# A two-branch mixer on one core: where V rows land, how the attention output comes back, who begins the first loads, and fused feature maps

## The chip, the cores and the metric

The kernel runs on one core of one Trainium2 chip. The metric is the device time of one execution in microseconds. A core has five instruction streams that run side by side and meet through semaphores: TensorE (PE, matmuls into PSUM), VectorE (DVE), ScalarE (ACT), GpSimd (POOL) and SyncE (SP), which in this kernel issues the DMAs.

## The reference

Two branches read the same input `x` of 2048 tokens by 512 channels, and a gate per token mixes them. Everything is bfloat16 at the borders.

```python
g = sigmoid((x * gate_w).sum(-1, keepdims=True))
a = A(x)          # 32 heads of 16, four segments of 512 tokens
b = B(x)          # a long convolution per channel
return g * a + (1 - g) * b

# A, for segment s of 4:  phi(t) = where(t > 0, t + 1, exp(t))
p     = softmax(q_s k_s^T * scale + causal_mask)
a_mem = (phi(q_s) @ M) / (phi(q_s) @ z + 1e-6)
o_s   = sigmoid(beta) * a_mem + (1 - sigmoid(beta)) * (p @ v_s)
M, z  = M + phi(k_s)^T v_s,  z + phi(k_s).sum()
# then all segments' o @ wo

# B:  K[d, l] = Re sum_n C[d,n] * exp(dt*A[d,n]*l) * dt*B[d,n]
y = irfft(rfft(x, 2L) * rfft(K, 2L))[:L] + x * Dskip
```

## The kernel before

The kernel is built by a planner in Python. Functions such as `project`, `group`, `ophase`, `oproj`, `tables` and `tail` hand operations to a class `Sched`, each with an engine, a modelled cost, the tiles that it reads and writes and a priority key. `Sched.schedule` then builds one fixed order for each engine: it takes, among the operations that could start now, the one with the lowest key. Keys come from the constants `KEYS` and, for single stages by name, from `ORDER`. Some PSUM evacuations may go to ScalarE or VectorE (`evac`, lines 264 to 273), and `PEN` is added to the key for VectorE; `MODEK` is added for a change of TensorE's tile shape. `VPK` is the packet count that the planner charges for a V transfer. `Sched.emit` writes the streams out, with a wait wherever one engine needs another's result. So a change of a constant can move any operation of the program.

Buffers are pools at fixed SBUF addresses with a phase number. Pools of different phases may overlap; a pool can be used once every overlapping pool of an earlier phase has given back all of its tiles.

The work, in its order:

- **Loads and prologue.** All DMAs are issued by SP, one after the other: the parameters of branch B, `x` of segment 0, then `wq`, `wk`, `wv`. TensorE transposes parameters and `x`; `ssm_prep` and `ssm_powers` build powers of exp(dt*A) on VectorE and ScalarE.
- **Attention, four segments of four head groups.** `project` makes q and k, `key_tokens` and `seg_state` the state M (with the feature map of k as two terms, min(exp, 1) and max(k, 0), that are both multiplied with v), `group` the masked softmax, `ophase` the normalised result, with the memory term from segment 1 on. For the last segment (`LATEO = 12`) the two terms of phi(q) are added inside `ophase` (line 1181). `oproj(s)` multiplies by `wo`, scales by the gate (lines 269 and 270), and writes four row blocks of 128 tokens to a DRAM scratch `scr_abuf`. Two buffers `ag` hold the rows on their way.
- **Tables of branch B.** `table_f` and `tables` (VectorE, lines 1250 to 1255) build the kernel K in the tiles `F` and `G` with a scratch `t2`; each chunk goes through a DRAM scratch `scr_K`.
- **Convolution.** `x_level1` does the first level of a transform of `x` and stores it in a DRAM scratch `scr_Z`; `tail` loads it as four tiles `Zx`. For each of 16 frequency groups t, `tail` loads constants `c_D` (tile `Dst`, five buffers), transforms K (matmuls from line 1333), transforms x (line 1344), multiplies on VectorE (lines 1351 to 1358), transforms back into a tile `V` (line 1366) and sends V by a DMA from SBUF to SBUF into eight partitions of the large tile `V2`. These are the "K steps".
- **Final stage.** For each of 16 output column blocks, six matmuls give the last level plus the skip term, and VectorE adds the gated attention tile `aj` (line 1395, `SCALAR_TENSOR_TENSOR`). `aj` is read back from `scr_abuf` in four loads of 512 KB. Five output writes follow.

The V transfer and the read-back, before:

```python
S.dma(lambda t=t: sbp(V2, t, 16, 8, [[1024, 16], [1, 1024]]), ...)      # partitions t, t+16, ..., t+112
S.dma(lambda aj=aj: ap(aj, n=2048),
      lambda gq=gq: bass.AP(abuf, gq * 2048, [[8192, 128], [1, 2048]]), ...)
```

Of the kernel before, what the change touches and what calls it, by code (L numbers as in the profile page):

```python
# [8 lines left out]
BF16 = mybir.dt.bfloat16  # L9
# [8 lines left out]
VPK = 1400  # L18
LATEM, LATEO = 24, 12
MODEK = 3.2  # L20
PEN = 8.8
SHOW = 0
KEYS = (11.73, 0.11, 49.7, 49.9, 6.68, 12.43, 50.14, 14.66, 16.9, 95.49, 11.41, 2.82)
NDST, NV = 5, 5
ORDER = {'grp0.3.1': 5.2, 'oph3.2': -34.8, 'ktok1.1': 7.8, 'grp0.0.0': 12.9, 'K1': 4.1, 'ktok2.0': -13.6, 'K8': -1.8, 'oph2.0': 21.1, 'grp0.0.1': 7.6, 'ktok2.1': -2.1, 'grp3.0.1': 8.5, 'grp3.3.1': -2.0, 'tabF': 3.5, 'tab3': 13.2, 'oph2.1': -3.4, 'oproj2': 9.3, 'oph3.3': -2.3, 'grp0.1.1': 0.3, 'tok3': -4.8, 'proj3.2': 0.5, 'proj2.2': -2.6, 'oph1.1': -20.1, 'grp3.1.0': 17.6, 'proj0.1': -9.4, 'state2': 38.3, 'ktok1.3': -3.1, 'state1': -12.4, 'oph1.0': 5.3, 'grp2.0.1': 0.6, 'oproj1': -9.3, 'proj1.1': -4.6, 'grp0.2.1': -1.7, 'K15': -3.7, 'ktok0.1': 1.3, 'proj1.3': -1.4, 'grp1.2.1': -8.6, 'grp3.0.0': 3.2, 'grp2.2.0': 3.1, 'proj3.0': -24.4}
# [109 lines left out]
class Op:  # L135
    __slots__ = ("eng", "cost", "fn", "deps", "key", "tiles", "wt", "nd", "succ", "start", "fin", "idx", "inc",
                 "val", "sem", "know", "waits", "seq", "lat", "alld", "tag", "alts", "pew", "mode", "base")


class Sched:  # L140
# [59 lines left out]
    def op(self, eng, cost, fn, r=(), w=(), pw=(), key=None, lat=None, acq=(), alts=None, pew=(), mode=None):  # L200
        o = Op()
        o.pew = pew
# [56 lines left out]
    def dma(self, out, in_, nbytes, r=(), w=(), pw=(), key=None, slow=False, packets=0):  # L259
        kw = {"allow_slow_non_contiguous": True} if slow else {}  # L260
        lat = max(nbytes / 290e3, packets * 0.0015)
        return self.op("SP", 0.4, lambda e: e.dma_start(out(), in_(), **kw), r=r, w=w, pw=pw, key=key, lat=lat)  # L262
# [178 lines left out]
    def emit(self):  # L441
# [49 lines left out]
        def make(e):  # L491
            def run(eng):
                for o in self.prog[e]:
# [8 lines left out]
                    if e == "SP":  # L502
                        ins.then_inc(dsem[o.sem[1]], 16)
                    elif o.inc:
                        ins.then_inc(sems[e], 1)
# [38 lines left out]
def fft_consts():  # L544
# [31 lines left out]
    for tp in range(32):  # L576
        for i in range(4):
            r = 16 * (4 * (tp % 2) + i) + tp // 2
# [31 lines left out]
def build_kernel(nc, A_x, A_wq, A_wk, A_wv, A_wo, A_beta, B_A_re, B_A_im, B_B_re, B_B_im,  # L610
                 B_C_re, B_C_im, B_log_dt, B_Dskip, gate_w, out):
    with contextlib.ExitStack() as es:
# [119 lines left out]
        DP = mkpool("Dst", 4096, NDST, 2)  # L732
        K3P = mkpool("K3", 2048, 3, 2)
        XsP = mkpool("Xs", 2048, 3, 2)
        YP = mkpool("Y", 2048, 3, 2)
        V2P = mkpool("V2", 32768, 1, 2)
        ZxP = [mkpool("Zx0", 8192, 1, 2)]
        VP = mkpool("V", 2048, NV, 2)
        assert a <= 207 * 1024, a
        a = A0  # L740
        ZxP += [mkpool("Zx1", 8192, 3, 2)] * 3
        TtP = mkpool("Tt", 2048, 2, 2)
        assert a <= E1, (a, E1)
        a = Q0
        ajP = mkpool("aj", 4096, 4, 2)
# [28 lines left out]
        for T, wsrc, ky in ((wqT, A_wq, 0.3), (wkT, A_wk, 0.4), (wvT, A_wv, 0.5), (woT, A_wo, 9.0)):  # L774
            S.dma(lambda T=T: ap(T, dims=[[512, 4], [1, 512]]), lambda wsrc=wsrc: wsrc.rearrange("(k p) n -> p k n", p=128),
                  524288, w=[T], key=ky)
# [10 lines left out]
        def do_xT(s):  # L787
# [4 lines left out]
                  524288, w=[xks], key=(-0.95 if s == 0 else S.key - 8))  # L792
# [102 lines left out]
        dA = [DT() for _ in range(16)]  # L895
# [85 lines left out]
        def key_tokens(s, hg):  # L981
# [10 lines left out]
            op("ACT", c_act(512), lambda e: e.activation(ap(ek, n=512), ap(P, n=512), ACT.Exp), r=[P], w=[ek])  # L992
            op("ANY", 0.0, None, r=[P], w=[rk], alts={
# [5 lines left out]
        def seg_state(s, hp):  # L999
# [3 lines left out]
            for _ in range(1):  # L1003
                P = S.ps()
                for h2 in range(2):
                    hg = 2 * hp + h2

                    def f(e, P=P, hg=hg, h2=h2):
                        for tb in range(4):
                            for wi in range(2):  # L1010
                                i = mm(e, ap(P, h2 * 136, n=136), ap(ekr[(s, hg)][wi], tb * 128, n=128),
                                       ap(vpad[s], tb * 544 + hg * 136, n=136), tb == 0 and wi == 0, tb == 3 and wi == 1)
                        return i
                    op("PE", c_mm(136, 8), f, r=[vpad[s]] + list(ekr[(s, hg)]), pw=[P], acq=[Mx[s + 1]])
# [10 lines left out]
        def project(s, hg):  # L1025
# [27 lines left out]
            if s > 0:  # L1053
                eq, rq = Tile(eqP, BF16), Tile(rqP, BF16)
                op("ACT", c_act(512), lambda e: e.activation(ap(eq, n=512), ap(qT, n=512), ACT.Exp), r=[qT], w=[eq])  # L1055
                op("DVE", c_ts4(512), lambda e: e.tensor_scalar_min(ap(eq, n=512), ap(eq, n=512), 1.0), w=[eq])
                op("DVE", c_ts4(512), lambda e: e.tensor_scalar_max(ap(rq, n=512), ap(qT, n=512), 0.0), r=[qT], w=[rq])
# [99 lines left out]
        def ophase(s, hg):  # L1157
# [18 lines left out]
            if s > 0:  # L1176
# [3 lines left out]
                if late:  # L1180
                    op("DVE", c_tt(512), lambda e: e.tensor_tensor(ap(eq, n=512), ap(eq, n=512), ap(rq, n=512), ALU.add), r=[rq], w=[eq])
# [30 lines left out]

        def oproj(s):
            S.tag = "oproj%d" % s
            ot = [oTs[(s, hg)] for hg in range(4)]
            for tb in range(4):
# [10 lines left out]
                S.dma(lambda tbg=tbg: abuf[128 * tbg:128 * tbg + 128, :], lambda ag=ag: ap(ag, n=512), 131072, r=[ag], w=[dA[tbg]])  # L1227
# [78 lines left out]
        def tail(k0):  # L1306
# [16 lines left out]
            for t in range(16):  # L1323
                S.key = k0 + 4 + KEYS[4] * t
                S.tag = "K%d" % t
                Dt = Tile(DP, BF16)
# [34 lines left out]
                V = Tile(VP, BF16)  # L1361
# [8 lines left out]
                S.dma(lambda t=t: sbp(V2, t, 16, 8, [[1024, 16], [1, 1024]]), lambda V=V: ap(V, n=1024), 262144, r=[V], pw=[V2], packets=VPK)  # L1370
            S.key = k0 + 80
            for gq in range(4):
                S.tag = "fin%d" % gq
                aj = Tile(ajP, BF16)
                S.dma(lambda aj=aj: ap(aj, n=2048), lambda gq=gq: bass.AP(abuf, gq * 2048, [[8192, 128], [1, 2048]]),
                      524288, r=dA, w=[aj], key=k0 + 50)
# [122 lines left out]
```

## Time and profile before

| | |
|---|---|
| median of 5 runs | 369.32 us (363.28 to 372.58) |
| the profiled execution | 372.88 us, span 371.1 us |
| busy: TensorE, VectorE, ScalarE, GpSimd | 317.7, 293.0, 270.3, 3.2 us |
| mean granted TensorE clock | 0.848 |
| bytes moved by DMA | 37.15 MB |
| final adds, line 1395 | 16, busy 10.6 us |

The profile's busy time says when an engine had an instruction in work. For TensorE it counts at whatever clock was granted, so 10 us at a clock of 0.5 hold the work of 5 us at full clock. In a wait, the name after the arrow is what ended the idle time. "SPq" is SP's instruction stream; its waits are DMAs that could not be issued yet. Nearly all matmuls go through one helper and carry line 761, and copies out of PSUM carry lines 266 and 267, so groups are told apart by time and shape rather than by line.

### The profile page before, as it was taken

The page shows a single profiled execution, that of the slowest core. Times are in us where ns is not written, and L with a number is a line of the kernel's source. Part 1 is how long each engine was busy: PE and PEld are TensorE (multiplying, and loading weights), DVE is VectorE, ACT ScalarE, POOL GpSimd, SP SyncE. Part 2 cuts the span into 40 slices and gives each one's busy share as a digit, 9 for nine tenths or more (in the row PEclk, how much of TensorE's full clock was granted, in tenths as well). Part 3 has the DMA queues.
Part 4 walks back from the last instruction along what each step waited for, and adds up shares of the span by engine and source line. Part 5 has one row for each costly group of instructions (what it writes and reads, how often), then busy time and mean ns, then how long its engine had stood idle before and what let it go on. Part 6 is the DMA issues. An engine that isn't in the chain of part 4 may idle for free.

```text
span 371.1 us, 12049 instructions
## 1 busy us (share of the span) xinstructions
PE 317.7 (86%) x5403; PEld 177.3 (48%) x5403; DVE 293.0 (79%) x516; ACT 270.3 (73%) x362; POOL 3.2 (1%) x9
## 2 busy tenths in 40 slices
PE   3856589989997979987987999979999999999591
PEld 3433344445454655465655756445544443444350
DVE  3899999999997859674994689846889789788255
ACT  3899998878978846794987588946866998767300
POOL 2000000000000000000000000000000000000000
PEclk9995655589969565799988599967999999999998
DMA  7931013453100021011200200427498735842574
GB/s 180 270 111 60 28 41 105 125 153 123 58 3 2 4 38 60 2 45 35 22 2 5 38 30 32 115 71 246 102 349 187 180 88 159 182 118 47 135 283 170
DMA packets 38082, 37.15 MB, mean 100 GB/s; under 512 B 16784, under 2 KB 32272, under 8 KB 38032
## 3 DMA queue, kind: packets, MB, share of 16 engines
q1 hardware_dynamic: 38032, 36.40, 35.4%
q8 instruction: 42, 0.69, 0.8%
q14 instruction: 8, 0.07, 0.1%
HBM read 23.15 MB, written 9.04 MB: 87 GB/s over the span
## 4 chain that ended last, share of the span: by engine, by line
PE 59%; DVE 21%; ACT 8%; issue 5%; DMA 4%; SPq 1%; DVEq 0%; ACTq 0%
PE psum L761 56%; DVE sb L267 4%; ACT sb L1110 3%; DVE sb L1250 3%; ACT sb L266 2%; DVE sb L1252 2%; DVE sb L1395 2%; DVE sb L1255 2%; DMA scr_abuf<-sb 2%; PE psum L1165 2%; DMA sb<-in_A_wq_dram 2%; SPq L262 1%; DVE sb L870 1%; DVE sb L869 1%; DMA sb<-scr_abuf 1%
## 5 line engine op out<-in xcount | busy, mean ns | idle before, releaser
L761 PE MATMUL psum<-sb 128*32 128x20 bf16 (+14 forms) x5139 | 297.1, 247 | 36.8 <-ACT sb L1110 12.0
L761 PEld LDWEIGHTS psum<-sb 128*128 128x128 bf16 (+6 forms) x5139 | 156.8, 102 | 174.4 <-issue 52.4
L1110 ACT ACTIVATE sb<-psum 128x1024 bf16<-128x1024 f32 (+1 forms) x160 | 144.3, 942 | 18.6 <-PE psum L761 17.1
L266 ACT ACTIVATE sb<-psum 128x512 bf16<-128x512 f32 (+3 forms) x118 | 88.5, 763 | 52.6 <-PE psum L761 46.4
L267 DVE CAST sb<-psum 128x512 bf16<-128x512 f32 (+2 forms) x56 | 47.6, 855 | 21.4 <-PE psum L761 21.0
L1255 DVE TENSOR_TENSOR sb<-sb 128x2048 bf16<-128x2048 bf16 (+4 forms) x27 | 30.8, 1140 | 0.7
L1250 DVE TENSOR_TENSOR sb<-sb 128x2048 bf16<-128x2048 bf16 (+4 forms) x27 | 30.8, 1139 | 0.5
L1252 DVE TENSOR_TENSOR sb<-sb 128x2048 bf16<-128x2048 bf16 (+4 forms) x27 | 30.6, 1132 | 0.1
L1395 DVE SCALAR_TENSOR_TENSOR sb<-psum,sb 128x512 bf16<-128x512 f32 x16 | 10.6, 743 | 8.7 <-DMA sb<-scr_abuf 8.7
L1050 DVE TENSOR_SCALAR sb<-sb 128x512 bf16<-128x512 bf16 x32 | 9.9, 349 | 5.9 <-ACT sb L266 5.6
L1358 DVE TENSOR_TENSOR sb<-sb 128x512 bf16<-128x512 bf16 x32 | 13.6, 425 | 1.1
L1165 PE MATMUL psum<-sb 128*128 128x128 bf16 x128 | 12.0, 248 | 0.8 <-ACT sb L266 0.8
L1351 DVE TENSOR_TENSOR sb<-sb 128x1024 bf16<-128x1024 bf16 x16 | 11.0, 686 | 1.8 <-ACT sb L266 1.8
L1173 DVE TENSOR_TENSOR sb<-psum,sb 128x512 bf16<-128x512 bf16 x16 | 11.1, 691 | 0.5
L1115 DVE TENSOR_TENSOR sb<-sb 128x512 bf16<-128x512 bf16 x24 | 9.7, 416 | 1.8 <-ACT sb L1110 1.8
L1353 DVE TENSOR_TENSOR sb<-sb 128x1024 bf16<-128x1024 bf16 x16 | 11.0, 685 | 0.0
L1165 PEld LDWEIGHTS psum<-sb 128*128 128x128 bf16 x128 | 9.3, 112 | 3.0 <-ACT sb L266 1.1
L800 PE MATMUL psum<-sb 128*128 128x128 bf16 x64 | 8.0, 300 | 1.6 <-DMA sb<-in_A_x_dram 1.6
L1055 ACT ACTIVATE sb<-sb 128x512 bf16<-128x512 bf16 x12 | 7.5, 634 | 2.0 <-PE psum L761 2.0
L267 DVE COPY sb<-psum 128x1024 bf16<-128x1024 bf16 (+1 forms) x8 | 4.8, 618 | 5.2 <-PE psum L816 4.8
L1195 DVE TENSOR_TENSOR sb<-psum,sb 128x512 bf16<-128x512 f32 x12 | 8.3, 691 | 0.4
L1170 DVE RECIPROCAL sb<-psum 128x32 f32<-128x32 bf16 x16 | 5.6, 352 | 3.7 <-PE psum L1165 3.6
(70 smaller groups left out, 145.8 us busy)
## 6 DMA issues: line engine op xcount, KB each, us to landing
sb<-c_D SPq DMA_DIRECT2D x16, 512.0 KB, 7.2
sb<-in_A_x_dram SPq DMA_DIRECT2D x8, 512.0 KB, 4.3
scr_Z<-sb SPq DMA_DIRECT2D x16, 256.0 KB, 2.2
sb<-scr_Z SPq DMA_DIRECT2D x4, 1024.0 KB, 7.0
sb<-sb SPq DMA_DIRECT2D x16, 256.0 KB
scr_abuf<-sb SPq DMA_DIRECT2D x16, 128.0 KB, 2.9
sb<-scr_abuf SPq DMA_DIRECT2D x4, 512.0 KB, 5.4
out_dram<-sb SPq DMA_DIRECT2D x3, 512.0 KB, 2.6
```

The lines of the kernel that those rows point to most:

```text
L266: fa = lambda e: e.activation(dst(), src(), ACT.Copy)
L267: fd = lambda e: e.tensor_copy(dst(), src())
L761: mm = lambda e, o_, l, r_, st, sp, **kw: e.matmul(o_, lhsT=l, rhs=r_, start=st, stop=sp, skip_group_check=True, **kw)
L1110: op("ACT", c_act(n), lambda e, P=P, pT=pT, sj=sj, n=n: e.activation(ap(pT, sj * 1024, n=n), ap(P, n=n) if n == 1024 else ap(P, dims=[[512 ...
L1165: i = e.transpose(ap(P, tb * 256 + gi * 128, n=128), ap(ra[gi], tb * 128, n=128), ap(ident, n=128))
L1173: op("DVE", c_dps(512), lambda e: e.tensor_tensor(ap(o1, dims=[[128, 4], [16, 8], [1, 16]]), ap(P, dims=[[256, 4], [32, 8], [1, 16]]), ap( ...
L1250: op("DVE", c_tt(2 * nc_ * n), lambda e: e.tensor_tensor(run(tile, ne, dst, 1), run(tile, ne, src, sstep), pwv(0), ALU.mult), r=rd + [pw], ...
L1252: op("DVE", c_tt(2 * nc_ * n), lambda e: e.tensor_tensor(run(t2, n, 0, 1), run(tile, ne, src, sstep), pwv(1), ALU.mult), r=rd + [pw], w=[t2])
L1255: op("DVE", c_tt(2 * nc_ * n), lambda e: e.tensor_tensor(D_(), D_(), ap(t2, 2 * n, [[4 * n, nc_ // 2], [-2 * n, 2], [1, 2 * n]]), ALU.add) ...
L1351: op("DVE", c_tt(1024), lambda e, Y=Y, Xs=Xs, K3=K3: e.tensor_tensor(ap(Y, dims=[[512, 2], [1, 512]]), ap(Xs, dims=[[512, 2], [1, 512]]), ...
L1358: op("DVE", c_tt(512), lambda e, Y=Y, Tt=Tt, co=co: e.tensor_tensor(ap(Y, co * 512, n=512), ap(Y, co * 512, n=512), ap(Tt, co * 512, n=512 ...
L1395: op("DVE", c_dps(512), lambda e, P=P, aj=aj, bl=bl, b4=b4: e.scalar_tensor_tensor(ap(aj, bl * 512, n=512), ap(P, n=512), ap(omg4T, b4, n= ...
```

## The change

There are six edits.

1. **V rows.** Step t's V goes to the eight partitions 32*(t//4) + t%4 + 4j instead of t + 16j. The constant `G2` is permuted to match. `VPK` goes from 1400 to 850.
2. **Attention output.** `aj` becomes one tile of 16 KB per partition, laid over the Z tables 1 and 2 once these are spent. Segments 0 to 2 still go through `scr_abuf` and are read back in three loads of 32 partitions. The four row blocks of segment 3 go from `ag` straight into eight partitions of `aj` each.
3. **First loads.** `x` of segment 0 and `wq` are issued by ScalarE's stream, ahead of everything else in it, instead of by SP.
4. **Fused late maps.** For segment 3's q, and for one key group (segment 2, head group 3), phi is built as min(exp(t), max(t + 1, 1)) in one tile. The add in `ophase` goes, and that key group's state takes four matmuls instead of eight.
5. **Final stage.** Of the 16 column blocks, four (`FINP`: 0, 4, 7, 8) are scaled and copied by ScalarE and added by GpSimd; the other twelve stay on VectorE. There are ten output writes instead of five.
6. **Layout and order.** The tail's pools are placed differently (two `Dst` buffers over `t2`, three over `G`, `V` and `Zx` split into several pools), and `KEYS`, `ORDER`, `PEN` and `MODEK` have new values.

```diff
-VPK = 1400
+FINP = (0, 4, 7, 8)
+LATEK = 11
+VPK = 850
-MODEK = 3.2
-PEN = 8.8
+MODEK = 2.7
+PEN = 14.1
...
-    def dma(self, out, in_, nbytes, r=(), w=(), pw=(), key=None, slow=False, packets=0):
+    def dma(self, out, in_, nbytes, r=(), w=(), pw=(), key=None, slow=False, packets=0, q="SP"):
...
+                if e == "ACT":
+                    mine = [o for o in self.prog["SP"] if o.q == "ACT"] + mine
+                elif e == "SP":
+                    mine = [o for o in mine if o.q == "SP"]
...
-            r = 16 * (4 * (tp % 2) + i) + tp // 2
+            t = tp // 2
+            r = 32 * (t // 4) + 4 * (4 * (tp % 2) + i) + t % 4
...
+        DP = [mkpool("Dst", 4096, 2, 2)] * 2 + [mkpool("Dst1", 4096, 3, 2)] * 3
...
-                  524288, w=[xks], key=(-0.95 if s == 0 else S.key - 8))
+                  524288, w=[xks], key=(-0.95 if s == 0 else S.key - 8), q="SP" if s else "ACT")
...
+            if 4 * s + hg >= LATEK:
+                op("DVE", c_dps(512), lambda e: e.tensor_scalar(ap(rk, n=512), ap(P, n=512), 1.0, 1.0, ALU.add, ALU.max), r=[P], w=[rk])
+                op("DVE", c_tt(512), lambda e: e.tensor_tensor(ap(ek, n=512), ap(ek, n=512), ap(rk, n=512), ALU.min), r=[rk], w=[ek])
+                ekr[(s, hg)] = (ek,)
+                return
...
-                if late:
-                    op("DVE", c_tt(512), lambda e: e.tensor_tensor(ap(eq, n=512), ap(eq, n=512), ap(rq, n=512), ALU.add), r=[rq], w=[eq])
...
+                    S.dma(lambda tbg=tbg: ap(ajs[0], p0=8 * tbg, np_=8, dims=[[512, 16], [1, 512]]), lambda ag=ag: ap(ag, n=512),
+                          131072, r=[ag], pw=[ajs[0]], packets=1500)
...
-                S.dma(lambda t=t: sbp(V2, t, 16, 8, [[1024, 16], [1, 1024]]), lambda V=V: ap(V, n=1024), 262144, r=[V], pw=[V2], packets=VPK)
+                S.dma(lambda t=t: sbp(V2, 32 * (t // 4) + t % 4, 4, 8, [[1024, 16], [1, 1024]]), lambda V=V: ap(V, n=1024), 262144, r=[V], pw=[V2], packets=VPK)
...
+            for i in range(3):
+                S.dma(lambda i=i: ap(aj, p0=32 * i, np_=32, n=8192), lambda i=i: bass.AP(abuf, i * 262144, [[8192, 32], [1, 8192]]),
+                      524288, r=dA[4 * i:4 * i + 4], pw=[aj], key=k0 + 50, packets=1600)
...
+                    if b4 in FINP:
+                        yp = Tile(ypP, BF16)
+                        op("ACT", c_act(512) + 0.09, lambda e, P=P, yp=yp, b4=b4: e.activation(
+                            ap(yp, n=512), ap(P, n=512), ACT.Copy, scale=ap(omg4T, b4, n=1)), r=[P, omg4T], w=[yp])
+                        op("POOL", 1.0, lambda e, yp=yp, b4=b4: e.tensor_tensor(
+                            ap(aj, b4 * 512, n=512), ap(aj, b4 * 512, n=512), ap(yp, n=512), ALU.add), r=[yp], w=[aparts[bl]])
...
-                nh = 2 if gq == 3 else 1
+                nh = 4 if gq == 3 else 2
```

## The prediction

> **What bounds the kernel now.** I read the busy rows and the slices first, then the busy time by stage, then the waits of the last 46 us, then the chain that ended last.
>
> ```profile
> PE 317.7 (86%) x5403; PEld 177.3 (48%) x5403; DVE 293.0 (79%) x516; ACT 270.3 (73%) x362; POOL 3.2 (1%) x9
> PEclk9995655589969565799988599967999999999998
> ```
>
> No engine is full on average, and TensorE's granted clock falls to half for long stretches. By stage (columns: stretch, length, busy us of PE, PEld, DVE, ACT, POOL, then granted clock, DMA share, GB/s):
>
> ```profile
> 10.00:20.00 10.00, 8.22 (x56) 4.39 (x56) 8.03 (x18) 8.68 (x16) 0.00 (x0) 1.00 0.97 257
> 30.00:40.00 10.00, 7.64 (x98) 4.65 (x94) 9.79 (x18) 9.80 (x15) 0.00 (x0) 0.50 0.20 65
> 140.00:160.00 20.00, 18.86 (x296) 10.02 (x294) 15.27 (x19) 14.36 (x20) 0.00 (x0) 0.68 0.09 29
> 280.00:300.00 20.00, 19.46 (x258) 8.22 (x256) 17.23 (x34) 16.08 (x20) 0.00 (x0) 1.00 0.75 183
> 345.00:352.00 7.00, 4.03 (x33) 2.50 (x32) 0.75 (x1) 1.71 (x2) 0.00 (x0) 1.00 0.57 136
> 357.00:367.00 10.00, 5.64 (x48) 3.70 (x48) 9.92 (x16) 0.00 (x0) 0.00 (x0) 1.00 0.69 273
> ```
>
> Four regimes: loads until about 12 us; VectorE and ScalarE full until about 80; TensorE full from 100 to 345, at full clock from 260; then a tail of 26 us in which TensorE works under half of the time. The waits of the tail (who, for whom: us in total, times, longest):
>
> ```profile
> DVE sb L1395 <- DMA sb<-scr_abuf: 8.7, 1, 8.7
> PE psum L761 <- DMA sb<-sb: 3.0, 1, 3.0
> ACT sb L269 <- DMA scr_abuf<-sb: 2.0, 1, 2.0
> ```
>
> The chain through it (start, us, what):
>
> ```profile
> 344.48 4.37 DMA scr_abuf<-sb
> 348.94 0.70 ACT sb L269
> 349.65 2.56 DMA scr_abuf<-sb
> 352.23 4.05 DMA sb<-scr_abuf
> ...
> 363.63 3.29 DVE sb L1395 x5
> ```
>
> The reader should see a round trip through DRAM between the last output projection and the final adds, 2.56 + 4.05 us, with every engine idle for most of it, and then 16 adds on VectorE, one every 0.664 us (10.63 us from 356.30). The span ends 4.15 us after the last add.
>
> [...]the V transfer issued at 334.73 stands alone on the queues from 336.0 to 338.4, and its five half-microsecond rates (two shown) add up to 252 KB.
>
> ```profile
> 337.00:337.50 0.50, 0.50 (x4) 0.26 (x3) 0.50 (x1) 0.26 (x1) 0.00 (x0) 1.00 0.46 160
> 337.50:338.00 0.50, 0.50 (x4) 0.21 (x3) 0.47 (x2) 0.00 (x0) 0.00 (x0) 1.00 0.52 168
> ```
>
> [...]
>
> **The change part by part.**
>
> *V rows.* [...]Fifteen of the sixteen transfers are covered by TensorE work, so their gain is nothing. The last is waited for: issued at 346.99, TensorE resumes at 351.84. [...]the adds wait later for the attention rows, so it counts only if those come earlier.
>
> *Attention rows.* The read-back of segments 0 to 2 moves under the K steps (three loads of 512 KB; the DMA share there is 0.54 to 0.77, so it fits). On SP they stand behind waits for the attention writes and for the Z tables' last use, and the spectrum and V transfers queue behind them; five spectrum buffers cover that. Segment 3 goes straight to SBUF: four transfers onto eight partitions each[...]. [...]about 2.2 around it (V issued 334.73, data from 336.0: 1.3; 0.9 taken for completion, rounded up: the last V's data end within 351 to 352 and its wait at 351.84). [...]ScalarE's evacuations wait for block 0 and 1 too, since there are two ag buffers.
>
> *Final adds.* Four of sixteen go to ScalarE (a scaled copy, 0.69 us as L269) and GpSimd. GpSimd's add isn't in the trace; [...]bounds 0.85 (the memset of 544 numbers) and 2. All four lie beside VectorE; SP's output writes go in order, so a late one would hold the others, which costs something only past 2 us. VectorE has 12 x 0.664 = 8.0 us, 2.6 less. The finer output writes (ten issues of 0.33 us, not five) are covered by the adds.
>
> *Tail, summed.* Old order: adds from 357.0, 8.0, and 4.15 after them: 369.1, a gain of 2.0. If the output projection comes some 5 us earlier, V2 decides: [...]TensorE then has 16 pairs of 512 columns at 0.43 (24 such matmuls took 5.14 us at 324.67) and the eight groups of four 128-column products that no free bank let it do before, at 0.22 (eight L1165 took 0.45): 8.7 us. The last add of 0.74 and 4.15 follow: 364.0, a gain of 7.1. The new order can't be read from the diff; I take about the middle, 4.5.
>
> *First loads.* SP issues wq as the tenth, at 6.15, and it lands at 11.74:
>
> ```profile
> 6.15 5.59 DMA sb<-in_A_wq_dram
> 11.78 1.05 PE psum L761 x4
> 12.86 0.60 ACT sb L266
> ```
>
> ScalarE's queue would begin it near 1.2 us; the two issues go ahead of a table load whose result is first used at 4.79, and SP is spared 0.50 + 0.91 us. But the DMA share is 0.97 from 10 to 20, so bytes are only reordered, and wk (landed 13.2) is next. What comes forward is bounded by the gaps that VectorE and ScalarE have there: 0.59 + 1.23 on ScalarE, 0.43 + 0.70 on VectorE. I take 1.5; bounds -0.5 (the parameter rows now share bandwidth) and 2.
>
> *Fused maps.* For segment 3 VectorE loses one 0.29 us instruction in each of four head groups, and a 0.42 us add leaves the path between projection and state product. One key map trades a ReLU for a longer VectorE pair and halves eight matmuls. TensorE is full there and covers all of it: 0.3 (0 to 1.2).
>
> *Buffers.* Two of five spectrum buffers move onto t2, free after the last table product (237.3) instead of after the table matmuls (246.9). So fewer bytes stand before the K write:
>
> ```profile
> 246.97 1.92 SPq L262 DMA_DIRECT2D sb<-c_D  x3
> 248.93 0.43 SPq L262 DMA_DIRECT2D scr_K<-sb  x1
> 249.79 1.43 SPq L262 DMA_DIRECT2D sb<-c_D  x2
> 256.89 2.58 SPq L262 DMA_DIRECT2D sb<-scr_K  x4
> ```
>
> That write took 7.9 us, against a median of 2.4, behind 2.5 MB. With 1 MB gone early it is some 3 us shorter and the K steps may begin sooner. TensorE is busy at half clock then, so I take 1 (0 to 3).
>
> *Order.* New penalties and keys reorder everything. Nothing in the trace prices that: plus or minus 5, taken as 0.
>
> Sum: 4.5 + 1.5 + 0.3 + 1 = 7.3. The profiled execution took 372.9 (span 371.1), so 365.6 for one like it; it is 3.6 over the median of 369.3, from which the gain gives **362.0**.
>
> **The rivals.** [...](0.20): the four SBUF transfers stand in file with V14 and V15, and the wait for DRAM becomes one for a queue. For it: the half share[...]. Against: an order with the projections earlier hides it. Gain 2.0 + 1.5, nothing else: 365.8.
> *Overlap* (0.24): the projections come early and the K steps start sooner, in the half-clock stretch at 246 to 255. For it: that stretch, and the 7.9 us write. Against: TensorE is busy in it. 7.1 + 2 + 3 = 12.1: 357.2.
> *Clock* (0.11), the slower one: in the new order the stretch from 160 to 200 loses its clock, as 140 to 160 has now. It did 17.7 us at 1.00 and 18.0 at 0.91, 34.1 of full clock; at 0.68 that is 50 us instead of 40. With 7.3 gained: 372.0. It decides once more than 7.3 us are lost, some 22 us of TensorE-bound work at 0.75 of the present clock. Against: VectorE fills half of these stretches.
> [...]
>
> **How the numbers follow.** Forecast 0.45 (own range 358 to 366), rivals 0.20, 0.24, 0.11. 2% of 369.3 is 7.4 us, about what a measurement of this kernel can tell from no change. Half of the forecast's chance and nearly all of the overlap's lie beyond it: faster 0.46. Slower by over 2% needs 376.7, about half of the clock case: 0.05. Same: 0.49. The range for 8 in 10: 354 to 370.
>
> **What would show it.** Right: no read-back in the tail; twelve final adds on VectorE that begin between 351 and 355 and last 8 to 9 us; [...]the first projection before 9 us; the K write landing in under 5 us. The queue rival shows as adds waiting for sb<-sb; the clock rival as a granted clock under 0.7 between 160 and 200. Wrong: adds that begin after 357, GpSimd adds of over 2 us that hold back output writes, or a mean clock below 0.82 (0.848 now).

## The result

| | before | changed |
|---|---|---|
| median | 369.04 us (71 executions, 361.17 to 378.68) | 362.52 us (36 executions, 359.96 to 368.21) |
| profiled execution | span 371.1 us, clock 0.848 | span 363.7 us (365.48 in all), clock 0.846 |

The ratio of changed to before is 0.9948, with a 95% interval of 0.9925 to 0.9971: 0.5% faster, some 2 us. Only executions within 1.5% of the fastest of their kernel enter the ratio, 24 of the 71 before and 31 of the 36 of the changed kernel, so it sets the best third of the one against nearly all of the other, and the medians lie further apart (6.5 us) than the ratio says.

The prediction named 362.0 us, and the median is 362.52. That is luck, not a confirmation. Against the best executions of the kernel before the gain is about 2 us, and the rest of the distance between the medians is the narrower spread of the changed kernel (8 us instead of 17), which no step of the prediction had. The terms of the sum, measured one by one below, don't add up to 7.3 us.

The busy row and the clock of the changed kernel's profile:

```profile
PE 313.7 (86%) x5399; PEld 173.6 (48%) x5399; DVE 285.9 (79%) x501; ACT 277.5 (76%) x373; POOL 7.8 (2%) x13
PEclk9995555579999956998775599959999999999968
```

TensorE lost 4 us of work and VectorE 7; ScalarE has 7 more. The stretches answer to those shown of before (the columns are the same; the kernel before had 0.91 as its clock from 180 to 200):

```profile
10.00:20.00 10.00, 9.76 (x66) 5.47 (x67) 8.86 (x20) 8.39 (x14) 0.00 (x0) 1.00 0.92 257
140.00:160.00 20.00, 19.79 (x335) 10.63 (x335) 18.24 (x25) 16.92 (x25) 0.00 (x0) 0.93 0.25 63
180.00:200.00 20.00, 16.21 (x557) 10.37 (x550) 13.27 (x23) 16.51 (x23) 0.00 (x0) 0.68 0.01 3
280.00:300.00 20.00, 19.71 (x227) 8.34 (x221) 14.77 (x28) 17.98 (x21) 0.00 (x0) 1.00 0.47 149
```

The low clock has moved: 140 to 160 has 0.93 now (0.68 before) and 180 to 200 has 0.68 (0.91 before). From 280 to 300 the DMA engines are busy 0.47 of the time instead of 0.75, with most of the traffic still there (149 GB/s instead of 183): a first hint of what the V rows do.

The waits of the tail, who, for whom, us in total, times, longest (window 320 to 364):

```profile
DVE sb L1440 <- DMA sb<-sb: 11.2, 1, 11.2
PE psum L779 <- DMA sb<-sb: 5.0, 1, 5.0
ACT sb L274 <- DMA sb<-sb: 1.8, 2, 0.9
```

And its chain (start, us, what):

```profile
338.51 1.03 ACT sb L271
...
339.56 6.13 DMA sb<-sb
...
345.74 8.96 PE psum L779 x52
...
354.72 4.81 DVE sb L1440 x7
```

No wait for `scr_abuf` is left: the read-back did leave the tail. But the last V, for which TensorE waited until 4.85 us after its issue before (346.99 to 351.84), takes 6.13 us here and 5.24 in a second profile, and behind it stand TensorE's matmuls instead of VectorE's adds. From the end of the last V evacuation to the end of the span it is 346.96 to 371.1 before, 24.1 us, and 339.54 to 363.7 now, 24.2 us; a second profile of each gave 24.0 (span 360.7) and 22.4 (span 362.1). So the tail gained 0 to 1.7 us, where the prediction had 4.5.

The two profiles of the kernel before end their last V evacuation at 346.96 and 336.67, ten microseconds apart with one and the same program. The changed kernel's are at 339.54 and 339.69, and the variants of it below that keep its order up to there lie between 337.7 and 340.8, except v_four_ports (343.4). What differs is the granted clock (the column after POOL's), here from 120 to 160 us in the two profiles of before:

```profile
120.00:160.00 40.00, 35.22 (x814) 21.57 (x807) 29.70 (x47) 27.67 (x38) 0.00 (x0) 0.66 0.11 24
```

```profile
120.00:160.00 40.00, 34.83 (x883) 23.04 (x884) 31.24 (x55) 29.80 (x41) 0.00 (x0) 0.81 0.13 31
```

From 200 to 260 it is 0.80 and 0.94. The two profiles of the changed kernel have 0.79 and 0.83, 0.85 and 0.84. Among 67 executions of the kernel before, timed together with before_again, the four shortest (360.64 to 361.42 us) had a mean clock of 0.875 or 0.876, and the four longest (374.27 to 376.45) one of 0.823 to 0.839. Why one program is steadier than the other stays open.

### The profile page after: what moved, and what is told of

Same layout as the page of the kernel before. It is cut to its first block, busy times and chain, and to the rows that moved or that the text cites. A ratio compares the mean times of both kernels' runs of the same rounds, so it can differ in the third digit from the quotient of the medians.

```text
span 363.7 us, 12053 instructions
## 1 busy us (share of the span) xinstructions
PE 313.7 (86%) x5399; PEld 173.6 (48%) x5399; DVE 285.9 (79%) x501; ACT 277.5 (76%) x373; POOL 7.8 (2%) x13
## 4 chain that ended last, share of the span: by engine, by line
PE 59%; DVE 15%; ACT 11%; DMA 7%; issue 5%; SPq 1%
PE psum L779 56%; ACT sb L1139 5%; DVE sb L272 4%; ACT sb L271 4%; DMA scr_K<-sb 2%; PE psum L1194 2%; DMA sb<-in_B_A_im_dram 2%; DMA sb<-sb 2%; DVE sb L1286 2%; DVE sb L1291 1%; DVE sb L1440 1%; DVE sb L1288 1%; SPq L265 1%; DMA sb<-scr_K 1%; PE psum L818 1%
## 5 line engine op out<-in xcount | busy, mean ns | idle before, releaser
L779 PEld LDWEIGHTS psum<-sb 128*128 128x128 bf16 (+6 forms) x5135 | 153.9, 101 | 171.9 <-issue 53.7
L1139 ACT ACTIVATE sb<-psum 128x1024 bf16<-128x1024 f32 (+1 forms) x160 | 143.8, 942 | 19.6 <-PE psum L779 18.4
L271 ACT ACTIVATE sb<-psum 128x512 bf16<-128x512 f32 (+4 forms) x116 | 88.0, 780 | 39.0 <-PE psum L779 32.3
L272 DVE CAST sb<-psum 128x512 bf16<-128x512 f32 (+2 forms) x61 | 50.5, 836 | 27.1 <-PE psum L779 26.5
L1440 DVE SCALAR_TENSOR_TENSOR sb<-psum,sb 128x512 bf16<-128x512 f32 x12 | 8.4, 750 | 13.7 <-DMA sb<-sb 11.2
L274 ACT ACTIVATE sb<-psum,sb 128x512 bf16<-128x512 f32 x14 | 9.6, 687 | 4.1 <-PE psum L779 2.2
L1387 DVE TENSOR_TENSOR sb<-sb 128x1024 bf16<-128x1024 bf16 x16 | 10.9, 684 | 0.8 <-ACT sb L271 0.8
L271 ACT ACTIVATE sb<-sb 128x512 bf16<-128x512 f32 (+2 forms) x16 | 11.0, 699 | 0.6 <-DVE sb L887 0.3
L1194 PE MATMUL psum<-sb 128*128 128x128 bf16 x128 | 11.2, 238 | 0.0
L1389 DVE TENSOR_TENSOR sb<-sb 128x1024 bf16<-128x1024 bf16 x16 | 10.9, 685 | 0.0
L1435 ACT ACTIVATE sb<-psum,sb 128x512 bf16<-128x512 f32 x4 | 2.7, 688 | 9.3 <-PE psum L779 9.3
L1220 DVE TENSOR_SCALAR sb<-psum 128x32 f32<-128x32 f32 x12 | 2.2, 187 | 8.9 <-PE psum L779 8.9
```

Source lines behind the costliest of these rows:

```text
L271: fa = lambda e: e.activation(dst(), src(), ACT.Copy)
L272: fd = lambda e: e.tensor_copy(dst(), src())
L779: mm = lambda e, o_, l, r_, st, sp, **kw: e.matmul(o_, lhsT=l, rhs=r_, start=st, stop=sp, skip_group_check=True, **kw)
L1139: op("ACT", c_act(n), lambda e, P=P, pT=pT, sj=sj, n=n: e.activation(ap(pT, sj * 1024, n=n), ap(P, n=n) if n == 1024 else ap(P, dims=[[512 ...
L1194: i = e.transpose(ap(P, tb * 256 + gi * 128, n=128), ap(ra[gi], tb * 128, n=128), ap(ident, n=128))
L1387: op("DVE", c_tt(1024), lambda e, Y=Y, Xs=Xs, K3=K3: e.tensor_tensor(ap(Y, dims=[[512, 2], [1, 512]]), ap(Xs, dims=[[512, 2], [1, 512]]), ...
```

## The experiments

Ratios are to the kernel before. "Tail" is the time from the end of the last V evacuation to the end of the span, in the profile of the run.

**Both kernels again** (before_again, after_again).

> The kernel before, once more, for a second profile of it. Theory 1 (the tail gives its gain back): the stretch from the end of the last V evacuation to the end of the span is again about 24 us, as in the first profile (346.96 to 371.1) and as in the changed kernel (339.54 to 363.7), and whatever separates this execution from the first one lies between 20 and 340 us, in stretches where the granted clock differs. Theory 2 (the tail is shorter in the changed kernel, and the middle eats it): the stretch is 24 us here too, but the K steps begin no later than in the changed kernel (257 us).

> The changed kernel, once more. Ratio to the kernel before 0.99 to 1.00. Theory 1: tail again about 24 us after the last V evacuation, with a wait of TensorE for V2 of 4 to 6 us and a granted clock of 0.5 after it. If the clock stays at 1.0 after the wait in this execution, the tail should be some 3 us shorter than 24.

before_again: 0.9987 (0.9935 to 1.0039). after_again: 0.9931 (0.9894 to 0.9967), median 362.14. The ratio stands; 0.5% is what there is to explain, and differences of 0.3% between single runs are no evidence.

**V rows back in their old places** (v_four_ports), every engine's order as in the changed kernel.

```diff
-  sbp(V2, 32 * (t // 4) + t % 4, 4, 8, [[1024, 16], [1, 1024]])
+  sbp(V2, t, 16, 8, [[1024, 16], [1, 1024]])
```

> The changed kernel with V's rows back at t + 16j[...] and G2 to match; every instruction, wait and place in the order is the same. Theory P[...]: [...]time up by 1 to 2.4 us. Theory E ([...]the V issued at 331.01 in the wide kernel still moved its data from 332.0 to 334.5): the wait for V2 stays at 5 to 6 us and the time within 0.5 us of the changed kernel.

1.0177 (1.0095 to 1.0259): some 2.3% slower than the changed kernel (1.0177 over 0.9948), more than any theory had. The chain of this run:

```profile
316.69 11.74 DMA sb<-c_D
...
343.42 8.70 DMA sb<-sb
```

A spectrum load of 512 KB takes 11.74 us and stops TensorE (4.5 us of waits, and half clock from about 327 to 334), and the last V takes 8.70 us instead of 5.2 to 6.1 (tail 26.9). The rates in the tail, where the last two V stand one behind the other in the queues, show what the rows do. First the changed kernel, then this run (last two columns: DMA share, GB/s):

```profile
341.50:342.00 0.50, 0.00 (x0) 0.00 (x0) 0.00 (x0) 0.00 (x0) 0.00 (x0) 1.00 0.52 197
342.00:342.50 0.50, 0.00 (x0) 0.00 (x0) 0.00 (x0) 0.49 (x1) 0.00 (x0) 1.00 0.52 201
```

```profile
348.00:348.50 0.50, 0.00 (x0) 0.00 (x0) 0.00 (x0) 0.00 (x0) 0.00 (x0) 0.50 0.54 102
349.00:349.50 0.50, 0.00 (x0) 0.00 (x0) 0.00 (x0) 0.00 (x0) 0.00 (x0) 0.50 0.52 98
```

At the same DMA share, 0.52 to 0.54, the new rows move 197 and 201 GB/s and the old ones 102 and 98. In this program, K steps and tail together, the new rows are worth some 2.3%.

**The new V rows in the kernel before, nothing else** (v_eight_in_before): the same two lines, the other way round, in the old program; its order does not change.

> The kernel before with one edit: V rows on 32*(t//4) + t%4 + 4j (and G2 to match), every engine's order as it was. Theory E[...]: the median time from issue to landing of the 512 KB spectrum loads falls from 8.0 us to about 5, the wait for V2 at the end stays near 4.9 us, the time from the last V evacuation to the end stays at 24 us, and the run is within 0.5% of the kernel before. Rival (a V transfer is twice as fast everywhere, so the last one too): the wait for V2 falls by 1.2 us, to about 3.7, and the run is 0.3 to 1% faster.

0.9994 (0.9942 to 1.0047). The landing of the spectrum loads (window 250 to 362; last column: median us) in before, in this run, in the changed kernel and in v_four_ports:

```profile
sb<-c_D SPq DMA_DIRECT2D x13, 512.0 KB, 8.2
```

```profile
sb<-c_D SPq DMA_DIRECT2D x11, 512.0 KB, 4.3
```

```profile
sb<-c_D SPq DMA_DIRECT2D x11, 512.0 KB, 5.3
```

```profile
sb<-c_D SPq DMA_DIRECT2D x11, 512.0 KB, 8.0
```

The new rows take 2.7 to 3.9 us off the median spectrum load, and in the old program TensorE waits for none: no gain. In the changed one it waits for two of them once V is back on the old rows. What took the slack there is not shown: the 1.5 MB of read-back in that stage, or the new order, or the new places of the buffers. From the end of its evacuation to TensorE's restart the last V took 4.22 us instead of 4.86 (before_again), half of the 1.2 that the rival has from halving the 2.4 us of the lone V; the adds waited for the attention rows in any case. So theory E holds, with that correction: the new rows bring the spectrum loads down, and the run gains nothing.

**The order and the parts, crossed** (old_order: the changed program with KEYS, ORDER, PEN and MODEK of before; new_order_only: the program before with those of the changed kernel).

> The changed code with KEYS, ORDER, PEN and MODEK of the kernel before (VPK stays at 850). So all new parts, in an order near the old one. If the new parts alone carry the gain (tail 24.1 to about 22.2 us), the ratio to the kernel before is 0.993 to 0.997, as for the changed kernel. If the retuned order carries it, the ratio is 1.00 or above.

> The kernel before with the four order constants of the changed one (KEYS, ORDER, PEN, MODEK), nothing else. Theory O (the constants are fitted to one program each, and are worth nothing apart from it): slower than the kernel before by 1 to 3%, as the changed program was with the old constants. Rival (the new order is what gains, and the new parts give nothing): faster than the kernel before by 0.5% or more, with the last V evacuation at 340 or earlier in its profile.

| | old constants | new constants |
|---|---|---|
| old parts | 1 | 1.0506 (1.0433 to 1.0579) |
| new parts | 1.0244 (1.0143 to 1.0344) | 0.9948 (0.9925 to 0.9971) |

Either half alone loses 2 to 5%. In the chains of both, old_order first, a slow spectrum load stands, as in v_four_ports:

```profile
334.39 12.84 DMA sb<-c_D
```

```profile
333.78 8.48 DMA sb<-c_D
```

But TensorE waits for such loads only 1.7 and 1.9 us in all, a small part of the 9 and 19 us that are lost. The losses lie ahead of the tail: the last V is issued at 356.97 and 355.12, and at 339.56 in the changed kernel and 346.99 and 336.70 in the two profiles of the kernel before. That the order is fitted to the moments at which one program's transfers meet is a guess that these loads suggest; the rest of the loss was not traced. What the table does show is that the order is not a term of its own that can be added to the others.

**Segment 3 through DRAM** (seg3_by_dram): the four row blocks go through `scr_abuf` again, in a fourth read-back, every other part new. The planner then builds another order for the tail.

```diff
-  if s < 3:
+  if True:
...
-  for i in range(3):
+  for i in range(4):
```

> The changed kernel with segment 3's four row blocks written to the DRAM scratch and read back as a fourth load of 32 partitions, as segments 0 to 2 are; the order before the tail is the same. Theory A (the round trip is what the change saves): the adds begin some 2 to 4 us later and the time rises by 2 to 3 us. Theory F (in the changed kernel V2 sets the tail[...]): [...]the wait for V2 after the last V evacuation falls from 6.1 or 5.2 to about 4.8, and the time stays within 1 us of the changed kernel.

0.9941 (0.9911 to 0.997), tail 23.0 us: in the whole, no difference from the changed kernel that these runs can measure. But the two differ in more than the direct write. TensorE's last work before its wait for V2, in the changed kernel and here:

```profile
337.43 3.26 PE L779 MATMUL psum<-sb 128*128 128x512 bf16 x20 [0.81 <-DVE sb L1394]
```

```profile
338.58 4.75 PE L779 MATMUL psum<-sb 128*128 128x512 bf16 x43 [0.82 <-DVE sb L1394]
```

Here eight groups of skip terms (32 products of 128 columns) stand ahead of V2, and in the changed kernel two (8 products). So this run is to be compared with f0_ahead below, which has eight as well and writes directly. From the end of the last V evacuation to the first add of VectorE it is 10.9 us here (340.68 to 351.62) and 9.3 there (339.40 to 348.68), the twelve adds take 7.99 us without a gap in both, and the tails are 23.0 and 21.4. By these two profiles the direct write is worth some 1.6 us in the tail, near the 2.0 that the prediction had for the tail in its old order; in the changed kernel the adds wait for TensorE, and it doesn't show.

**Segment 3's blocks on 32 partitions** (wide): tokens dealt out so that the blocks cover partitions 96 to 127, 32 each instead of 8.

```diff
-  ap(ajs[0], p0=8 * tbg, np_=8, dims=[[512, 16], [1, 512]])
+  ap(ajs[0], tb * 512, [[2048, 4], [1, 512]], p0=96, np_=32)
```

> The changed kernel with segment 3's output projection taking every fourth token instead of 128 neighbours, so that each of its four row blocks is spread over 32 partitions[...] instead of 8[...]. The gate column for these blocks is built beside the old one (16 one-column matmuls and one small reciprocal more). Nothing else moves. Theory 1 (V14 and V15 stand in file behind the row blocks[...]): the wait for V2 falls from 6.1 us after the last V evacuation to about 3.5, TensorE idles some 2.5 us instead of 5 and keeps its clock, the tail after the evacuation goes from 24.2 to 18 to 19 us, the time falls by about 5 us (ratio to the changed kernel 0.986). Rival (the transfers do not disturb each other; the last V is slow by itself): wait stays near 6, gain below 1 us.

1.0023 (0.9988 to 1.0059), tail 23.1. From 342.5 to 343 the queues now move 299 GB/s at a DMA share of 1.11 (213 at 0.55 in the changed kernel), yet V2 lands 6.09 us after its issue, as in the changed kernel. That speaks against the narrow blocks as the reason for the 6.13 us there. Why the whole is slower than the changed kernel was not found; its profile is not (span 362.6).

**TensorE kept busy** (warm): 22 matmuls of 512 columns into a spare bank, during the wait for V2.

> The changed kernel with 22 matmuls of 512 columns more on TensorE, whose result nobody reads, between the last output projection and the first matmul that waits for V2 (4.7 us of work in a wait of 5). Every other instruction and its order are the same. Theory 1 (the clock that falls in this wait sets the tail): the 88 matmuls after the wait take about 10.3 us at full clock (32 x 0.214 + 56 x 0.056 = 10.0) instead of 13.0, the clock shows 1.0 throughout, and the time falls by 2.5 to 3 us (ratio to the changed kernel 0.992). Rival (attention rows and adds set it: twelve adds of 0.664 after the rows land at 348.5, or GpSimd and the output writes): no change, within 0.5 us.

0.994 (0.9905 to 0.9976), tail 22.0, V2 6.42 us. The clock is 1.00 throughout, and 86 matmuls after V2 take 10.52 us instead of 13.00 for 88; but V2 is what they wait for, and it came later.

**Skip terms ahead of V2** (f0_ahead): the planner is told that the last V comes late, so eight groups of four 128-column products stand ahead of the wait instead of two. **Both** (f0_ahead_warm): with ten matmuls of 512 columns as well.

```diff
-  ..., r=[V], pw=[V2], packets=VPK)
+  ..., r=[V], pw=[V2], packets=VPK if t < 15 else 4000)
```

> The changed kernel with eight skip-term groups ahead of the wait for V2 instead of two, and no matmuls to keep TensorE busy. Theory T: 24 products of 0.056 us go from behind the wait to before it, 1.3 us at full clock; after the wait the clock is at half for some 3 us; from the last V evacuation to the end about 21.5 us, ratio 0.990. Rival (only the clock counts, and idle time still takes it): 22.4 us or more, ratio 0.994.

> The changed kernel with the planner told that the last V comes late, so that eight of the sixteen skip-term groups (four 128-column products each) stand ahead of the wait for V2 instead of two, and with ten 512-column matmuls into a spare bank ahead of them, so that TensorE is not idle. Theory T (after V2 the tail is bound by TensorE, cold and with skip terms to do): V2 still lands 5 to 6 us after the last evacuation, then sixteen matmuls at 0.214 go at once; the adds are released by the last row block of segment 3 at about 348.5 and last 8.5 us; the time from the last V evacuation to the end falls from 22.4-24.2 to about 21; ratio to the kernel before 0.989. Rival (the adds are bound by the row blocks of segment 3 and by VectorE, 12 x 0.66 us): nothing changes, 22 us or more, ratio 0.993.

f0_ahead: 0.9948 (0.9879 to 1.0016), tail 21.4. f0_ahead_warm: 0.9863 (0.9801 to 0.9925), tail 21.6, median 361.22. VectorE in the tail of f0_ahead, then TensorE and VectorE in that of f0_ahead_warm:

```profile
348.68 7.99 DVE L1441 SCALAR_TENSOR_TENSOR sb<-psum,sb 128x512 bf16<-128x512 f32 x12 [11.42 <-DMA sb<-sb]
```

```profile
344.69 9.04 PE L781 MATMUL psum<-sb 128*128 128x512 bf16 x64 [1.36 <-DMA sb<-sb]
347.96 7.99 DVE L1450 SCALAR_TENSOR_TENSOR sb<-psum,sb 128x512 bf16<-128x512 f32 x12 [11.60 <-DMA sb<-sb]
```

Now the twelve adds run without a gap, 7.99 us, from the landing of segment 3's last row block on, in both runs: VectorE is the bound that the prediction took it for, and the last of the transfers onto eight partitions is what releases it. The ten matmuls show no gain of their own. The ratio of f0_ahead_warm is the lowest of all. But two runs below with the same tail (x_by_sp 21.5, k_write_first 21.4) have 0.9924 and 0.9931: that these edits beat the kernel before is sure, that they beat the changed one is shown by the tail, 0.8 to 2.8 us shorter, and not by the ratios.

**All adds on VectorE**, once in the changed kernel (final_adds_vector) and once in f0_ahead_warm (f0_warm_vector).

```diff
-FINP = (0, 4, 7, 8)
+FINP = ()
```

> The changed kernel with FINP empty: all sixteen final adds on VectorE, none on ScalarE and GpSimd, everything before the final stage as it was. Theory T (the final stage of the changed kernel is bound by TensorE, which needs 13 us for its 88 matmuls after V2): the adds fill the gaps that VectorE had, 16 x 0.664 = 10.6 us from 348.6 to 359.2 against 359.5 now; the ratio to the kernel before stays at 0.993-0.995. Rival (VectorE was the bound, as the prediction's sum of 12 x 0.664 supposes): 2.6 us longer, ratio 1.001.

> f0_ahead_warm with all sixteen final adds on VectorE. Theory T (with the skip terms done early and the clock up, VectorE is the bound from 348 on): adds 348.0 to 358.6 instead of 356.0, 2.6 us longer, from the last V evacuation to the end about 24.2 us, ratio 0.993. Rival (TensorE still bounds it): under 1 us longer, ratio 0.988.

The adds, in final_adds_vector and then in f0_warm_vector:

```profile
349.23 10.63 DVE L1440 SCALAR_TENSOR_TENSOR sb<-psum,sb 128x512 bf16<-128x512 f32 x16 [11.15 <-DMA sb<-sb]
```

```profile
347.89 10.63 DVE L1450 SCALAR_TENSOR_TENSOR sb<-psum,sb 128x512 bf16<-128x512 f32 x16 [11.56 <-DMA sb<-sb]
```

In the changed kernel with all adds on VectorE (ratio 0.9984, 0.9923 to 1.0044, too wide to decide) they end 19.6 us after the last V evacuation (359.86 less 340.22). With the adds shared out it is 20.0 and 18.2 in the two profiles: no gain from sharing can be told there. In f0_warm_vector they end at 358.52, 20.0 us after it, instead of 355.95, 17.4 us: there the same edit is worth 2.6 us (spans 362.7 and 360.1; too few executions for a ratio), and f0_ahead, x_by_sp and k_write_first below, whose adds are shared out too, have 17.3. The 2.6 of the prediction was right in size, and hidden.

**The two tail edits with wide blocks** (best_tail: f0_ahead_warm and wide together).

> The same, and segment 3's row blocks are dealt to 32 partitions each (token 4i + block in partition 96 + i), as in the run named wide. Theory T: blocks no longer hold the adds, which begin at about 346.8; from the last V evacuation to the end about 20 us; but the run named wide was 0.9% slower than the changed kernel for a reason not yet known, so the ratio is 0.990 if that reason is the tail, 0.999 if it lies before it. Rival: as before, 22 us, ratio 1.000.

Tail 19.7, the shortest of all, with adds from 345.48 on, and a span of 358.2; but the ratio is 0.9927 (0.9886 to 0.9968), no better than the changed kernel. The tail did what theory T said; what wide costs is not in it, as in the run wide, and stays open.

**Who begins the first loads** (loads_by_sp: `x` and `wq` back on SP in their old places, everything else new; x_by_sp: f0_ahead_warm with `x` on SP as its third DMA, so that only `wq` is begun by ScalarE).

> The changed kernel with x of segment 0 and wq issued by SP again, in their old places (third and tenth). All other instructions and their order stay. Predicted theory: the first loads by ScalarE are worth 1.5 us, so this is 1 to 2 us slower. Rival (the two loads take the bandwidth of the parameter rows, which landed at 5.84 and 7.95 instead of 4.14 and 7.05, and ScalarE's first copy began at 6.49 instead of 4.79): no slower, up to 1 us faster.

> f0_ahead_warm, with x of segment 0 issued by SP as its third DMA, as in the kernel before, and only wq begun by ScalarE. Theory H (x on a second queue takes bandwidth from A_re, so that the transposes start 1.6 us later than in the kernel before, which eats what wq gains): A_re lands near 4.5 us instead of 5.8, the first projection still before 11, and the instruction VectorE L963 or its like, at 22.8 to 22.9 in the changed kernel, comes at about 22; ratio 0.984. Rival (the head is bound by the sum of the bytes until 13 us, whoever issues them): L963 within 0.3 us of 22.8, ratio 0.986.

loads_by_sp had six executions, 357.38 to 372.28, too few and too wide for a ratio; in its profile the last V evacuation ends at 337.69, earlier than in the changed kernel, so in that profile a later head did not make the end later. x_by_sp: 0.9924 (0.986 to 0.9987). The head can be read from one small instruction of the chain there (start, us), in before, changed, loads_by_sp and x_by_sp:

```profile
22.57 0.16 DVE L945 TENSOR_SCALAR sb<-sb 128x4 f32<-128x4 f32 x1
```

```profile
22.83 0.16 DVE L963 TENSOR_SCALAR sb<-sb 128x4 f32<-128x4 f32 x1
```

```profile
23.94 0.17 DVE L963 TENSOR_SCALAR sb<-sb 128x4 f32<-128x4 f32 x1
```

```profile
22.86 0.16 DVE L967 TENSOR_SCALAR sb<-sb 128x4 f32<-128x4 f32 x1
```

loads_by_sp has it 1.1 us later than the changed kernel, but this instruction lies between 21.88 and 23.77 in the twelve profiles that have the new order and the changed kernel's first loads, so 23.94 is hardly clear of their scatter. Against the kernel before, which has it at 22.57 and 21.55, the loads by ScalarE bring nothing. In the changed kernel `wq` comes earlier, with the first projection at 10.24 instead of 11.78 (11.28 in loads_by_sp), and the parameters later: A_re lands at 5.84 instead of 4.14. With `x` back on SP it still lands at 5.42. That the bytes bound the head, whoever issues them, fits all this and is not shown.

**The K write first** (k_write_first: f0_ahead_warm, with the last K write on SP ahead of the four spectrum loads that preceded it).

> f0_ahead_warm with the last K write issued ahead of the four spectrum loads that stood before it on SP; every other engine's order as it was. The write should land in about 2.5 us instead of 7.9. Theory B (TensorE has other work there, and waits for the K reads only 0.7 us): K steps begin at most 0.7 us earlier, ratio 0.984 to 0.987. Rival (the K write sets when the K steps begin, as the buffers term of the prediction had it): 3 to 5 us, ratio 0.976.

The chain of the changed kernel there, then of f0_ahead_warm, from which this run differs by the one edit, then of this run:

```profile
243.48 7.88 DMA scr_K<-sb
...
253.32 3.89 DMA sb<-scr_K
...
257.25 4.94 PE psum L779 x25
```

```profile
236.60 16.60 PE psum L781 x215
...
256.24 5.79 PE psum L781 x29
```

```profile
236.85 17.66 PE psum L788 x224
254.51 0.45 PE psum L1203 x8
254.96 2.34 PE psum L788 x38
257.30 0.20 issue
257.50 4.71 PE psum L788 x24
```

The write is issued at 239.5 and has landed by 242.0; in f0_ahead_warm it took 7.4 us, and yet no DMA stands in the chain there either, only TensorE. The K steps begin at 257.50 instead of 256.24, not earlier, and the ratio is 0.9931 (0.9894 to 0.9967). In the changed kernel TensorE waited 0.7 us for the K reads; it had other work for all the rest.

## Why the prediction was wrong, step by step

- **Tail, 4.5 us: the term that was mis-sized.** It measured 0 to 1.7. The 4.5 was the middle between 2.0, for the old order, and 7.1, for an order in which the output projection comes some 5 us earlier and V2 decides. The projection did not come earlier: its last row block is issued at 342.72, 3.2 us after the last V (339.56), and in the kernel before at 349.65, 2.7 us after it (346.99). And the branch in which V2 decides was priced too short. It had 3.4 us from the issue of the last V to its landing, an estimate of the author with a shorter data phase that no trace of before showed; it took 6.13 (5.24 in the second profile). And it had 8.7 us for TensorE after it, with eight skip groups done early, as in the kernel before, at full clock. Only two groups stand ahead of V2 in the new order, and the clock is at 0.50 from about 344.2 to 351.0, so that 88 matmuls took 13.00 us (12.14 in the second profile). VectorE's adds, released by the last row block at 348.56 (predicted: 351 to 355), wait for them and end at 359.53, after 11 us (9.0 in the second profile; predicted: 8 to 9). The 4.17 us after the last add are the 4.15 predicted. With eight groups ahead of V2 the adds no longer wait for TensorE, and the tail is 21.4 to 21.6 in four profiles: 2.4 to 2.7 shorter than before, little more than the 2.0 of the old order. The prediction asked what would be late next and priced the row blocks and the adds, and looked at TensorE only as it stood in the old order.
- **The queue rival** was right in kind: in the changed kernel the DMA share stays between 0.50 and 0.57 from 341.5 to 344, with V15 and row blocks on their way. Which engines carry them is not shown. Blocks 0 and 1, issued at 335.69 and 336.51, run at 50 to 90 GB/s ahead of V14 and V15, which could explain the 6.13 us; but wide has 6.09 without such blocks, and a second profile of the changed kernel 5.24 with them, so what sets it stays open. From 344.5 to 345.5, where block 2 should stand, the rate is 45 to 51 GB/s, at which its 128 KB would take an estimated 2.6 to 2.9 us. As a rival it had the whole at 365.8, with adds from 357.0; they began 8 us sooner, so as a forecast of the end it was wrong.
- **V rows: "fifteen of the sixteen are covered, so their gain is nothing".** True of the kernel before (0.9994) and false of the changed one (2.3%). That the new rows shorten a transfer was the author's estimate; no trace of before shows it. The step priced an edit against the traffic and the order of the old program, which other edits of the same change replace; the read-back under the K steps is one that may spend the room that this one makes. That "five spectrum buffers cover that" was right with the new rows and wrong with the old.
- **One measured time was no evidence.** The lone V of before, with its data from 336.0 to 338.4, was taken to show that the rows bound a transfer: the author's estimate, which these runs don't bear out. With the new rows a lone V in the run wide, issued at 331.01, still moves from 332.0 to about 334.5, and its two highest rates are little above the 160 and 168 GB/s of before:

```profile
333.50:334.00 0.50, 0.50 (x4) 0.25 (x3) 0.50 (x2) 0.00 (x0) 0.00 (x0) 1.00 0.50 176
334.00:334.50 0.50, 0.50 (x4) 0.23 (x2) 0.47 (x2) 0.44 (x1) 0.00 (x0) 1.00 0.47 180
```

  The lone transfers took the same time on either rows, 2.4 and 2.5 us; one behind another they move 200 GB/s with the new rows and 100 with the old.
- **First loads, 1.5 us:** nothing against the kernel before. The prediction wrote that bytes are only reordered, took a gain anyway, and was right in its first sentence. The first projection came at 10.24, not before 9.
- **Fused maps, 0.3 us:** too small for these runs; not tried alone.
- **Buffers, 1 us:** nothing. Two spectrum loads went early, at 230.70 and right after it, as forecast; but all the other three are issued just before the K write, as three were in the kernel before, and it took 7.88 us again (predicted: under 5). The 2.5 MB that the prediction put before the write hold two loads that are issued after it; with four loads behind it, in k_write_first, it landed within 2.6 us. Even that gains nothing.
- **Order, 0 plus or minus 5:** the crossing shows that it has no value of its own; without its parts it costs some 19 us, and the parts without it 9.
- **Clock rival:** its sign came, a clock under 0.7 from 180 to 200 (0.75 from 160 to 200, and 0.68 in the second profile), but 140 to 160 got its clock back, the mean (0.846) did not move, and the kernel was not slower. **Overlap rival:** the K steps begin at 257.25, between the two profiles of before (about 263 and 253, the ten microseconds of the clock again), so the runs don't show it.
- **GpSimd's add** took 1.16 us (predicted bounds: 0.85 and 2), and in f0_ahead VectorE's twelve adds beside four of them 7.99, 0.666 each, as against 0.664 for sixteen without them (final_adds_vector). SP's output writes waited for it three times, at most 1.6 us; the last of them waits for VectorE.

## What to carry to other kernels

Price an edit in the program as it will be after the other edits of the same change: the V rows were worth nothing in the old program and 2.3% in the new one. And look at what a planner does with an edit before two runs are compared: the run through DRAM had another order of TensorE, which hid what it was to measure. After a wait is removed, recount all engines behind it in the new order, TensorE's leftover products and its clock too, before the next bound is named. One measured number that equals an estimate doesn't show the mechanism; vary the thing that the mechanism depends on.

## What the runs showed of the hardware

- A V transfer of 256 KB onto eight partitions took about 2.5 us alone, with the old rows (before, 336.0 to 338.4) as with the new (wide, 332.0 to 334.5), at a DMA share of 0.46 to 0.52 in the half-microseconds of its highest rates; one behind another, V moved at 100 GB/s with the old rows (v_four_ports) and 200 with the new (changed kernel). What the lone one waits for stays open.
- The rows of the V transfers also set how soon other transfers land, though these go to all partitions: spectrum loads of 512 KB landed in 8.0 to 8.2 us (median) beside V on the old rows (before, v_four_ports) and in 4.3 to 5.3 beside V on the new (v_eight_in_before, changed kernel).
- A wait of TensorE of 5.04 us in the changed kernel was followed by a granted clock of 0.50, which outlasted it by 5 us; a wait of 2.69 us in seg3_by_dram was followed by half clock too, and so were two of 0.86 and 1.56 us with 0.47 us of matmuls between them in f0_ahead, but not one of 2.97 us in the kernel before (1.00 up to 358). What length of wait it takes is not shown. With matmuls in the wait the clock stayed at 1.00 (warm).
